# One written list for the first two units: sums, operands and combinations as steps of their own

## The chip, the cores and the metric

The kernel runs on one core of one Trainium2 chip. The metric is device time in microseconds, the median of three runs. A core has a matrix engine (TensorE, PE in the profile), a vector engine (VectorE, DVE), a scalar engine (ScalarE, ACT), a general engine (GpSimd, POOL) and a sync engine (SyncE, SP) whose queue issues most of the DMA transfers here. Each engine takes its instructions in the order in which the program lists them, and waits on semaphores where it needs another engine's result.

## The reference

Retention attention over 8 batches, 8 heads, 576 positions and head size 64, then an RMS norm and a SwiGLU feed-forward layer on the 4608 tokens of width 512 with inner width 1536, all in float32:

```python
scores = scale * np.matmul(q, k.transpose(0, 1, 3, 2))
Dmat = np.where(rel >= 0, gamma[:, None, None] ** rel[None, :, :], 0.0)
attn = np.matmul(scores * Dmat[None, :, :, :], v)
x = attn.transpose(0, 2, 1, 3).reshape(B * S, H * D)
rms = np.sqrt(np.mean(x * x, axis=-1, keepdims=True) + 1e-06)
xn = x / rms * rms_g
g = xn @ w_gate
out = (g * (1.0 / (1.0 + np.exp(-g))) * (xn @ w_val)) @ w_out
```

## The kernel before

**Units.** The 4608 tokens are worked in nine units of 512 (`NU`). Attention is done in 32 jobs, one for each batch and pair of heads; four jobs make a batch. Units 2 to 8 come from a loop after `start()`; units 0 and 1, with the loading, the attention of the first batches and the preparation of the weights, come from a list written out by hand, the string `PLAN`. `start()` first issues the loads in the order of `LOADS` (all on SP's queue), then walks through the list: `for step in PLAN.split(): tasks[step[0]](int(step[1:]))`. A step emits its instructions to whatever engines it uses; so the list sets the order on every engine, and nothing else does.

**Steps of the list.** For attention: `T` turns q and k of a job (transposes on PE, copies on ACT), `V` scales v, `S` is a job's slot (scores, states, weighing and, for the job before it, the outputs), `C` closes the last one, `P` and `F` prepare and fetch later jobs. For the norm: `Q` squares, `G` gathers, `N` the mean squares on PE (L454), `D` diagonals on ACT, `X` the `rb` matmul (L519) and four scalings on DVE (L521); for unit 2 `R`, `Y`, `X`, `M`: the `ms` matmul (L477), a root on ACT and DVE (L483 to L502), L521, and the four sums of x on DVE (L533) that the unit's second product needs (y, L614). For the weights: they come as 64-bit words and are brought to float32 in 36 halves; `a` is one exponent operation on ACT, `w` one step of a half (three DVE operations L1061, L1065, L1069, then a join L1086 on DVE); `W36` runs this to its end. Before slot 8 stands such a `W36`.

**The up projection.** `Uukn` is four 128x512 matmuls (L674) of unit u, set k, part n, followed by a silu on ACT or, for odd k, a multiply on DVE (L680). `d` makes two blocks of differences of h for the down projection on DVE (L698).

**The down projection.** `across(u)` multiplies h by the output weights with seven block products instead of eight, and each product again by seven. It is a generator: a first step that sets up, then for each product n an early step (three of the seven sub-products, with blocks taken from h directly, L773) and a late step (the other four), which needs four inner sums of that product's operand. After the late step the results in PSUM are kept (ACT, L788 and L790) or added (DVE, L800, L796) to the four output parts in `vec`. `A0` and `A1` each take one step of `across(0)` and `across(1)`.

**Inner sums.** `inner_sums(u, n)` makes them with four operations of 128x384 (L738, then three at L743), on POOL except where `on_vector` says DVE: products 4, 7, 10 and 12 when the two units' products are counted through as 7u + n. The buffer alternates with 7u + n, so the sums of a product can only start to overwrite when the late step two products earlier has been done. Before, those of product 7u + n + 2 are emitted by `across` itself, after the late step of product n and its adds; only products 0 and 1 of unit 0 are steps of the list, `i0` and `i1`.

**Operands and combination.** Two operands of the seven are sums of 128x1536 on DVE: the second and the last. Unit 0's are emitted at L937 and L943 behind its products 0 and 3, unit 1's at L955 and L957 behind unit 0's products 3 and 6. When unit 0 has had its seven products, its four output parts are combined at L977 by seven operations on all parts at once: parts 0 and 1 on DVE, 2 and 3 on POOL, 128x256 each. `o0` then stores unit 0's output (eight DMAs of 128 KB on SP).

Of the kernel before, what the change touches and what calls it, by code (L numbers as in the profile page):

```python
# [41 lines left out]
def kernel(  # L42
# [683 lines left out]
        at = (0, 1, None, 0, 1, 0, 1)[n] if u > 1 else (7 * u + n) % 2  # L726
        return [inner[:, at, i] for i in range(4)]

    def inner_sums(u, n, part=None):
# [4 lines left out]
        i1, i3, i2, i4 = inner_of(u, n)
        on_vector = u < 2 and 7 * u + n in (4, 7, 10, 12) or (u, n) == (NU - 1, 2)
        eng = nc.vector if on_vector else nc.gpsimd
        if part != 1:
            eng.tensor_tensor(out=i1, in0=x12, in1=x11, op=ALU.subtract)  # L738
        c = slice(1, NK) if part == 1 else slice(0, 1) if part == 0 else slice(0, NK)
        for o, a, b, op in (  # L740
            (i3, x22, x12, ALU.subtract), (i2, i3, x11, ALU.add), (i4, x21, i2, ALU.subtract),
        ):
            eng.tensor_tensor(out=o[:, c], in0=a[:, c], in1=b[:, c], op=op)  # L743
# [226 lines left out]
    def combine(b, eng=nc.vector):  # L970

        t = vec[:, b] if isinstance(b, slice) else vec[:, b : b + 1]
        for o, x, y in (
# [3 lines left out]
            eng.tensor_tensor(out=t[:, :, o], in0=t[:, :, x], in1=t[:, :, y], op=ALU.add)  # L977
# [147 lines left out]
    PLAN = """
        a1 a1 a1 a1 a1 T0 V0 S0 T1 V1 S1 a1 V2 T2 a1 Q0 V3 S2 G0 T3 Q1 a1 w1 a1 a1 S3 V4 a1 G1
        T4 w1 a1 S4 a1 a1 w1 a1 Q2 a1 a1 V5 T5 Q3 S5 G2 w1 V6 G3 w1 T6 S6 Q4 N0 D0 G4 V7 Q5 w1
        w1 T7 a1 a1 a1 X0 a1 G5 F8 S7 Q6 w1 U000 w1 G6 w1 C7 a1 a1 a1 a1 Q7 a1 G7 a1 a1 a1 a1 a1
        a1 w1 a1 a1 U001 N1 a1 a1 w1 U002 D1 w1 w1 U003 a1 w1 a1 X1 w1 w1 w1 U100 w1 w1 a1 U101
        a1 w1 w1 a1 a1 w1 a1 a1 w1 U010 w1 a1 U102 a1 w1 U103 a1 a1 w1 a1 w1 a1 w1 U011 a1 a1 w1  # L1130
        a1 w1 a1 w1 a1 a1 U012 w1 a1 w1 a1 w1 w1 a1 a1 U013 w1 a1 w1 U110 w1 w1 w1 U111 a1 a1 a1
        w1 a1 a1 w1 w1 a1 a1 w1 w1 a1 w1 U112 a1 a1 a1 a1 U020 a1 U113 a1 a1 a1 a1 a1 w1 w1 w1
        a1 U021 a1 w1 w1 a1 w1 w1 w1 U022 w1 a1 U120 w1 a1 w1 a1 a1 a1 w1 w1 w1 U121 a1 a1 U122
        a1 w1 U023 a1 U123 a1 w1 a1 a1 P8 a1 a1 a1 w1 w1 a1 a1 a1 w1 w1 w1 U030 w1 U031 F9 w1 a1
        w1 w1 a1 w1 U032 U130 a1 w1 a1 a1 U033 w1 w1 w1 a1 a1 a1 w1 a1 w1 w1 a1 w1 a1 U131 P9 a1
        a1 U132 a1 w1 U133 a1 w1 w1 w1 w1 w1 w1 U040 a1 U041 F10 w1 a1 w1 a1 a1 a1 a1 a1 a1 w1
        a1 U042 a1 w1 w1 a1 a1 a1 w1 U043 a1 w1 a1 a1 U050 a1 w1 w1 a1 a1 U051 U052 w1 w1 w1 w1
# [165 lines left out]
```

## Time and profile before

| what | value |
|---|---|
| runs | 1114.51, 1111.59, 1113.73 us, median 1113.73 |
| profiled execution | 1115.65 us, of which the span is 1113.8 |
| mean granted TensorE clock | 0.995 |
| instructions in the span | 24383 |
| HBM read, written | 212.05 MB, 30.08 MB |

The stretches by engine, from the table of windows of the profile: time in us that each engine was busy in each 25 us, with PE's granted clock.

| window, us | PE | DVE | ACT | POOL | PEclk |
|---|---|---|---|---|---|
| 0-25 | 20.25 | 10.27 | 12.41 | 0.87 | 1.00 |
| 25-50 | 20.35 | 18.10 | 14.85 | 0.35 | 0.93 |
| 50-75 | 24.39 | 20.07 | 14.48 | 5.96 | 0.93 |
| 75-100 | 24.16 | 16.53 | 14.94 | 6.37 | 1.00 |
| 200-225 | 23.70 | 23.33 | 6.31 | 13.77 | 1.00 |
| 250-275 | 25.00 | 22.58 | 5.00 | 18.02 | 1.00 |
| 275-300 | 23.69 | 21.64 | 4.13 | 19.62 | 1.00 |
| 300-325 | 24.09 | 17.79 | 4.04 | 13.22 | 1.00 |
| 350-375 | 23.01 | 16.38 | 4.11 | 5.93 | 0.93 |

The list's part takes the first 311 us or so: attention of the first batch and the loads up to about 58 us, the up projection of units 0 and 1 with the rounding of the weights and the slots of the second batch up to 240 us, unit 0's down projection from 240 to 278 us and unit 1's from 278 to 311 us. From there on the loop runs unit after unit. A window's busy time below 25 is time in which that engine stood still.

### The profile page before, as it was taken

How to read it: one execution, taken by the hardware profiler on the slowest of the kernel's cores; microseconds unless marked ns; L12 is line 12 of the kernel's file. 1: busy time of each engine (PE TensorE's matmuls, PEld its weight loads, DVE VectorE, ACT ScalarE, POOL GpSimd, SP SyncE). 2: the span in 40 equal slices, each digit the busy share in tenths (PEclk: the TensorE clock that was granted, in tenths of full speed). 3: DMA queues.
4: the chain of work that ended last, by engine and by line, in shares of the span. 5: the costliest groups of instructions: out<-in, count | busy, mean ns of one | idle time of the engine just before them, and what ended most of it. 6: DMA issues, size and time to landing. Idle time of an engine off the chain costs nothing.

```text
span 1113.8 us, 24383 instructions
## 1 busy us (share of the span) xinstructions
PE 1092.8 (98%) x10102; PEld 916.3 (82%) x10102; DVE 798.5 (72%) x1367; ACT 279.6 (25%) x565; POOL 467.6 (42%) x419
## 2 busy tenths in 40 slices
PE   8899999999999999999999999999999999999998
PEld 7654444469987899889988898889888998898888
DVE  4777767889867786688767785779476935594456
ACT  5557465211121220222022202131122111211110
POOL 0023535557730278025812382229312941393236
PEclk9899999999999999999999999999999999999999
DMA  7765889598778866787869865898485755575461
GB/s 183 202 183 198 307 210 258 196 330 227 235 286 225 189 224 244 214 223 212 290 166 215 275 251 171 245 229 293 154 216 199 248 208 177 171 287 169 157 245 42
DMA packets 253870, 243.72 MB, mean 219 GB/s; under 512 B 193088, under 2 KB 213824, under 8 KB 247616
## 3 DMA queue, kind: packets, MB, share of 16 engines
q1 hardware_dynamic: 252752, 241.87, 70.7%
q8 instruction: 79, 1.29, 0.5%
q10 hardware_dynamic: 1008, 0.30, 0.1%
q14 instruction: 31, 0.25, 0.1%
HBM read 212.05 MB, written 30.08 MB: 217 GB/s over the span
## 4 chain that ended last, share of the span: by engine, by line
PE 90%; DVE 5%; SPq 2%; issue 1%; POOL 1%; ACT 1%; DMA 0%; POOLq 0%; DVEq 0%; ACTq 0%
PE up L674 14%; PE x L614 13%; PE w L614 13%; PE z L614 13%; PE y L614 7%; PE xo L773 6%; PE xp L773 4%; PE zo L773 3%; PE zp L773 3%; PE yo L773 2%; PE wo L773 2%; PE av L355 2%; PE s L285 2%; PE av L375 2%; PE yp L773 1%
## 5 line engine op out<-in xcount | busy, mean ns | idle before, releaser
L674 PE MATMUL up<-x,ring 128*128 128x512 f32 x384 | 166.9, 594 | 1.3 <-DVE x L521 0.8
L614 PE MATMUL x<-x,ring 128*128 128x256 f32 x672 | 161.7, 384 | 0.0
L614 PE MATMUL w<-sums,ring 128*128 128x256 f32 x672 | 158.9, 379 | 0.0
L738 POOL TENSOR_TENSOR vi<-h 128x384 f32<-128x384 f32 x32 | 38.9, 1217 | 285.5 <-DVE h L633 270.2
L614 PE MATMUL z<-x,ring 128*128 128x256 f32 x672 | 158.8, 379 | 0.0
L674 PEld LDWEIGHTS up<-x,ring 128*128 128x128 f32 x384 | 72.4, 190 | 90.5 <-issue 84.1
L614 PEld LDWEIGHTS z<-x,ring 128*128 128x128 f32 x672 | 127.8, 190 | 19.8 <-issue 2.9
L614 PEld LDWEIGHTS w<-sums,ring 128*128 128x128 f32 x672 | 127.8, 190 | 17.2
L614 PEld LDWEIGHTS x<-x,ring 128*128 128x128 f32 x672 | 125.9, 191 | 17.5 <-issue 0.3
L743 POOL TENSOR_TENSOR vi<-h 128x384 f32<-128x384 f32 (+2 forms) x46 | 48.0, 1043 | 149.6 <-DVE h L633 149.6
L977 POOL TENSOR_TENSOR vi<-vi 128x512 f32<-128x512 f32 (+2 forms) x63 | 71.9, 1153 | 35.4 <-DVE vi L800 32.6
L640 ACT COPY m<-x 128x512 f32<-128x512 f32 x42 | 24.6, 585 | 231.1 <-PE x L614 231.1
L614 PE MATMUL y<-sums,ring 128*128 128x256 f32 x336 | 80.5, 383 | 0.9 <-DVE sums L533 0.9
L614 PEld LDWEIGHTS y<-sums,ring 128*128 128x128 f32 x336 | 64.7, 193 | 10.3 <-PE x L614 1.3
L621 DVE TENSOR_TENSOR h<-u,w 128x512 f32<-128x512 f32 x42 | 28.9, 688 | 58.5 <-PE w L614 58.2
L621 DVE TENSOR_TENSOR u<-m,y 128x512 f32<-128x512 f32 x42 | 28.7, 684 | 49.9 <-PE y L614 45.2
L635 ACT ACTIVATE h<-h 128x512 f32<-128x512 f32 x63 | 39.5, 629 | 82.1 <-DVE h L621 82.1
L334 DVE SCALAR_TENSOR_TENSOR sum<-sum,gc,s 128x64 f32<-128x64 f32 x192 | 53.9, 281 | 6.8
L1097 POOL TENSOR_TENSOR vi<-vi 128x512 f32<-128x512 f32 (+1 forms) x24 | 40.8, 1698 | 40.7 <-DVE vi L1086 26.8
L743 POOL TENSOR_TENSOR vi<-vi,h 128x384 f32<-128x384 f32 (+2 forms) x46 | 48.8, 1061 | 3.6
L743 POOL TENSOR_TENSOR vi<-h,vi 128x384 f32<-128x384 f32 (+2 forms) x46 | 46.2, 1005 | 3.6
L1097 POOL TENSOR_TENSOR ring<-ring 128x512 f32<-128x512 f32 x24 | 30.4, 1272 | 41.1 <-DVE ring L1086 30.7
(310 smaller groups left out, 2047.7 us busy)
## 6 DMA issues: line engine op xcount, KB each, us to landing
ring<-w_out_blocks SPq DMA_DIRECT2D x59, 1344.0 KB, 6.7
ring<-w_up_blocks SPq DMA_DIRECT2D x42, 1792.0 KB, 7.6
w_out_blocks<-vi SPq DMA_DIRECT2D x21, 448.0 KB, 4.5
out_dram<-vi SPq DMA_DIRECT2D x64, 128.0 KB, 3.1
qraw<-in_q_dram SPq DMA_DIRECT2D x96, 72.0 KB, 4.3
kraw<-in_k_dram SPq DMA_DIRECT2D x96, 72.0 KB, 3.4
k<-in_k_dram SPq DMA_DIRECT2D x48, 128.0 KB, 2.9
v<-in_v_dram SPq DMA_DIRECT2D x48, 128.0 KB, 3.1
```

The source lines that it names most:

```text
L285: nc.tensor.matmul(s[e][side(odd), i * L : i * L + L], lhsT=d["kT"][side(e), c * L : c * L + L], rhs=d["qT"][side(e), c * L : c * L + L], ...
L334: nc.vector.scalar_tensor_tensor(out=t[:, c], in0=t[:, c - 1], scalar=gc[:, hp : hp + 1], in1=part, op0=ALU.mult, op1=ALU.add,)
L614: nc.tensor.matmul(ps[:, i * HU : i * HU + HU], lhsT=w[:, PLACE[blk], c, i * P : i * P + P], rhs=t_of[u][blk][:, c], start=(start and i == ...
L621: nc.vector.tensor_tensor(out=o, in0=a, in1=pairs_of(ps), op=ALU.add)
L635: nc.scalar.activation(out=o, in_=c, func=AF.Silu)
L640: nc.scalar.copy(out=s1, in_=pairs_of(x_))
L674: nc.tensor.matmul(ps, lhsT=w[:, PLACE[blk], c % 2, i * P : i * P + P], rhs=x_of[u][:, c], start=(c == 0), stop=(c == NHP - 1),)
L738: eng.tensor_tensor(out=i1, in0=x12, in1=x11, op=ALU.subtract)
L743: eng.tensor_tensor(out=o[:, c], in0=a[:, c], in1=b[:, c], op=op)
L773: nc.tensor.matmul(ps, lhsT=lhs[:, c], rhs=w[:, s, c], start=((nm, s // 4) not in first), stop=False, skip_group_check=True,)
L977: eng.tensor_tensor(out=t[:, :, o], in0=t[:, :, x], in1=t[:, :, y], op=ALU.add)
L1097: nc.gpsimd.tensor_tensor(out=t[o], in0=t[x], in1=t[y], op=op)
```

## The change

What `across` emitted of its own for the first two units becomes steps of the list. `i` and `j` are now the inner sums of product n, counted 7u + n, on POOL and on DVE; `b0` and `b2` are the second operand of units 0 and 1, `b1` and `b3` the last one; `c` and `v` combine one output part of unit 0 on POOL and on DVE, with 128x128 operations. `combine` stores only where `late` is given, and `inner_sums` takes its engine as an argument; the work of units 2 to 8 is the same as before.

In the new list the inner sums of products 2, 6, 7, 8, 9, 10 and 11 are on DVE, those of 0, 1, 3, 4, 5, 12 and 13 on POOL. Parts 2, 0 and 3 of unit 0's output are combined on POOL, in this order, part 1 on DVE. Together DVE gains 12 operations of 128x384, and seven combining operations there are 128x128 instead of 128x256; POOL has 21 of 128x128 in place of seven of 128x256, and 12 inner sums fewer.

All other steps are set in a new order as well: the V, T, S steps of the first jobs, the U steps of both units, the a and w steps (two `a` fewer and one `w` more in the list, with the same instructions in all), the slots 8 to 11 against U043, U053 and U14n, and R2, Y2, X2, M2 of unit 2, where R2 stands after an early step instead of a late one's end. The loads have a new order too. In the diff the middle of both lists is left out.

```diff
@@ -726,14 +726,12 @@
         at = (0, 1, None, 0, 1, 0, 1)[n] if u > 1 else (7 * u + n) % 2
         return [inner[:, at, i] for i in range(4)]
 
-    def inner_sums(u, n, part=None):
+    def inner_sums(u, n, part=None, eng=nc.gpsimd):
 
         x = operands_of(u)[order_of(u)[n]]
         x11, x12 = x[:, :NK, :P], x[:, :NK, P:]
         x21, x22 = x[:, NK:, :P], x[:, NK:, P:]
         i1, i3, i2, i4 = inner_of(u, n)
-        on_vector = u < 2 and 7 * u + n in (4, 7, 10, 12) or (u, n) == (NU - 1, 2)
-        eng = nc.vector if on_vector else nc.gpsimd
         if part != 1:
             eng.tensor_tensor(out=i1, in0=x12, in1=x11, op=ALU.subtract)
         c = slice(1, NK) if part == 1 else slice(0, 1) if part == 0 else slice(0, NK)
@@ -741,6 +739,14 @@
             (i3, x22, x12, ALU.subtract), (i2, i3, x11, ALU.add), (i4, x21, i2, ALU.subtract),
         ):
             eng.tensor_tensor(out=o[:, c], in0=a[:, c], in1=b[:, c], op=op)
+
+    def second_operand(u):
+        o = operands_of(u)
+        nc.vector.tensor_tensor(out=o[S2], in0=o[A11], in1=o[S3], op=ALU.add)
+
+    def last_operand(u):
+        o = operands_of(u)
+        nc.vector.tensor_tensor(out=o[A22], in0=o[A12], in1=o[S2], op=ALU.subtract)
 
     def across(u):
 
@@ -882,7 +888,7 @@
                 inner_sums(u, n, part)
         if last:
             nc.vector.tensor_tensor(out=operands[S2], in0=b12, in1=b11, op=ALU.add)
-            inner_sums(u, 2)
+            inner_sums(u, 2, eng=nc.vector)
             nc.vector.tensor_tensor(out=operands[A22], in0=b21, in1=operands[S2], op=ALU.subtract)
         yield
         banks_in_turn = "zywxzwz" if u == 1 else "xxywzx." if last else "xzxzywx"
@@ -928,19 +934,21 @@
                 elif n == 4:
                     add(3, 3, "z")
                     add(2, 1, "z")
-                    combine(3)
+                    combine(3, late=True)
                 elif n == 5:
                     add(2, 2, "x")
-                    combine(2, nc.gpsimd)
+                    combine(2, nc.gpsimd, late=True)
             elif n == 0:
                 keep(1, "x")
-                nc.vector.tensor_tensor(out=b11, in0=b12, in1=b11, op=ALU.add)
+                if u:
+                    second_operand(u)
             elif n == 1:
                 keep(3, "z", -1.0)
             elif n == 2:
                 keep(0, "x")
             elif n == 3:
-                nc.vector.tensor_tensor(out=t1, in0=b21, in1=b11, op=ALU.subtract)
+                if u:
+                    last_operand(u)
             elif n == 4:
                 add(1, 1, "y")
                 add(2, 1, "z")
@@ -950,24 +958,15 @@
                 add(1, 1, "w")
             elif n == 6:
                 add(1, 1, "x")
-            o = operands_of(1)
-            if (u, n) == (0, 3):
-                nc.vector.tensor_tensor(out=o[S2], in0=o[A11], in1=o[S3], op=ALU.add)
-            elif (u, n) == (0, 6):
-                nc.vector.tensor_tensor(out=o[A22], in0=o[A12], in1=o[S2], op=ALU.subtract)
             if u > 1:
                 ahead = {0: 3, 1: 4, 2: 6, 3: 5} if last else {0: 3, 1: 4, 3: 5, 4: 6}
                 if n in ahead:
                     inner_sums(u, ahead[n])
-            elif 7 * u + n + 2 < 14:
-                inner_sums(*divmod(7 * u + n + 2, 7))
             yield
-        if not last:
-            if u == 0:
-                combine(slice(0, 2))
-            combine(slice(2, 4) if u == 0 else slice(0, 4), nc.gpsimd)
-
-    def combine(b, eng=nc.vector):
+        if u and not last:
+            combine(slice(0, 4), nc.gpsimd)
+
+    def combine(b, eng=nc.vector, late=False):
 
         t = vec[:, b] if isinstance(b, slice) else vec[:, b : b + 1]
         for o, x, y in (
@@ -975,7 +974,7 @@
             (S3, S1, S3), (A22, A11, A22),
         ):
             eng.tensor_tensor(out=t[:, :, o], in0=t[:, :, x], in1=t[:, :, y], op=ALU.add)
-        if not isinstance(b, slice):
+        if late:
             store(NU - 1, b)
 
     CORNERS = {A12: (0, 0), S4: (0, 1), S3: (1, 1), A22: (1, 0)}
@@ -1123,26 +1122,27 @@
     PLAN = """
-        a1 a1 a1 a1 a1 T0 V0 S0 T1 V1 S1 a1 V2 T2 a1 Q0 V3 S2 G0 T3 Q1 a1 w1 a1 a1 S3 V4 a1 G1
-        T4 w1 a1 S4 a1 a1 w1 a1 Q2 a1 a1 V5 T5 Q3 S5 G2 w1 V6 G3 w1 T6 S6 Q4 N0 D0 G4 V7 Q5 w1
-        w1 T7 a1 a1 a1 X0 a1 G5 F8 S7 Q6 w1 U000 w1 G6 w1 C7 a1 a1 a1 a1 Q7 a1 G7 a1 a1 a1 a1 a1
-        a1 w1 a1 a1 U001 N1 a1 a1 w1 U002 D1 w1 w1 U003 a1 w1 a1 X1 w1 w1 w1 U100 w1 w1 a1 U101
...
-        U053 a1 w1 w1 w1 a1 w1 a1 U140 W36 S8 a1 a1 a1 P10 U141 a1 S9 a1 a1 U142 F11 A0 a1 U143
-        a1 a1 a1 a1 z0 a1 d0 r1 a1 a1 a1 i0 d1 a1 S10 a1 a1 a1 P11 a1 a1 a1 U150 U151 a1 U152
-        S11 Q8 r2 U153 a1 i1 a1 d5 a1 d2 r99 A0 A0 A0 d3 C11 A0 A0 d4 G8 Q9 G9 A0 a1 A0 Q10 A0
-        k0 F12 G10 A0 A0 A0 a1 P12 A0 a1 A0 A0 F13 A0 Q11 G11 A1 A1 A1 o0 A1 A1 A1 A1 A1 A1 R2
-        A1 A1 A1 Y2 X2 M2 A1 a1 A1 A1 A1
+        V0 T0 a1 a1 a1 S0 T1 V1 a1 S1 T2 V2 a1 a1 V3 w1 S2 w1 Q0 T3 Q1 a1 G0 S3 a1 a1 V4 T4 a1
+        G1 a1 S4 a1 T5 a1 Q2 w1 G2 V5 w1 V6 Q3 S5 T6 a1 G3 a1 Q4 w1 V7 w1 S6 w1 F8 G4 N0 w1 a1
+        a1 D0 a1 T7 w1 a1 a1 a1 a1 X0 S7 a1 a1 a1 Q5 G5 w1 a1 Q6 G6 U000 a1 C7 Q7 w1 w1 a1 G7
+        U001 a1 N1 a1 w1 a1 D1 w1 w1 U002 a1 a1 a1 w1 a1 a1 a1 X1 w1 w1 w1 w1 a1 U003 a1 a1 a1
+        U100 w1 a1 w1 a1 w1 w1 w1 a1 w1 a1 a1 a1 a1 U110 a1 a1 w1 U101 w1 U010 w1 w1 w1 a1 w1 a1
...
+        U140 w1 a1 a1 a1 w1 a1 w1 a1 a1 a1 w1 a1 U043 U053 W36 S8 P10 U141 S9 a1 U150 a1 U142
+        F11 a1 a1 d0 a1 a1 Q8 z0 i0 a1 a1 U143 a1 S10 r1 a1 a1 U151 P11 U152 S11 U153 a1 d1 i1
+        d2 a1 a1 a1 Q9 r2 A0 r99 A0 A0 j2 A0 G8 a1 a1 d3 b0 d4 C11 A0 i3 A0 d5 a1 A0 a1 F12 A0
+        G9 b1 i4 Q10 k0 Q11 a1 b2 A0 i5 A0 a1 a1 G10 A0 j6 A0 A0 A0 a1 P12 A0 j7 b3 A0 j8 c2 A1
+        c0 F13 A1 v1 A1 c3 A1 j9 o0 G11 A1 A1 j10 A1 A1 j11 A1 i12 A1 R2 A1 Y2 A1 X2 M2 a1 a1
+        i13 A1 A1 A1 A1
     """
     TAILS = ((0, range(2)), (0, range(2, H)), (1, range(2)), (1, range(2, H)))
-    LOADS = [("table", 3), ("tails", 0), ("job", 0), ("job", 1), ("tails", 1), ("job", 2), ("job", 3), ("tails", 2), ("half", 0), ("job", 4), ("tails", 3), ("half", 1), ("job", 5), ("job", 6), ("half", 2), ("job", 7), ("half", 3), ("half", 4), ("rms_g", 0), ("table", 4)]
+    LOADS = [("tails", 0), ("job", 0), ("job", 1), ("tails", 1), ("tails", 2), ("job", 2), ("table", 3), ("job", 3), ("half", 0), ("half", 1), ("job", 4), ("tails", 3), ("job", 5), ("job", 6), ("job", 7), ("half", 2), ("half", 3), ("rms_g", 0), ("table", 4), ("half", 4)]
     stores = []
     n_joined = 0
     due = False
@@ -1222,7 +1222,11 @@
             "P": prepare, "F": fetch, "Q": lambda j: squares.append(squared(*divmod(j, NHP))),
             "G": lambda j: gather(*squares.pop(0)), "N": norm_1, "D": diagonals, "X": norm_2,
             "w": weights, "a": act, "d": lambda f: differences(f // 3, 2 * (f % 3)),
-            "i": lambda n: inner_sums(0, n), "z": lambda n: store_blocks(len(halves) + 9),
+            "i": lambda n: inner_sums(*divmod(n, 7)),
+            "j": lambda n: inner_sums(*divmod(n, 7), eng=nc.vector),
+            "c": lambda b: combine(b, nc.gpsimd), "v": combine,
+            "b": lambda n: (second_operand, last_operand)[n % 2](n // 2),
+            "z": lambda n: store_blocks(len(halves) + 9),
             "r": refill, "W": weights_to, "A": lambda u: next(outs[u], None), "R": root_1,
             "Y": root_2, "M": sums_of_x, "o": store,
             "k": lambda _: nc.vector.tensor_scalar(
```

The list without its a and w steps, from unit 0's last up products on, before:

```
U040 U041 F10 U042 U043 U050 U051 U052 U053 U140 W36 S8 P10 U141 S9 U142 F11 A0 U143 z0 d0 r1
i0 d1 S10 P11 U150 U151 U152 S11 Q8 r2 U153 i1 d5 d2 r99 A0 A0 A0 d3 C11 A0 A0 d4 G8 Q9 G9 ...
```

and after:

```
U040 F10 U133 U041 U042 U050 U051 U052 U140 U043 U053 W36 S8 P10 U141 S9 U150 U142 F11 d0 Q8 z0
i0 U143 S10 r1 U151 P11 U152 S11 U153 d1 i1 d2 Q9 r2 A0 r99 A0 A0 j2 A0 G8 d3 b0 d4 C11 A0 ...
```

More of the change, by code (lines that the diff above doesn't have):

```diff
@@ L1125 @@
     PLAN = """
-        a1 a1 a1 a1 a1 T0 V0 S0 T1 V1 S1 a1 V2 T2 a1 Q0 V3 S2 G0 T3 Q1 a1 w1 a1 a1 S3 V4 a1 G1
-        T4 w1 a1 S4 a1 a1 w1 a1 Q2 a1 a1 V5 T5 Q3 S5 G2 w1 V6 G3 w1 T6 S6 Q4 N0 D0 G4 V7 Q5 w1
-        w1 T7 a1 a1 a1 X0 a1 G5 F8 S7 Q6 w1 U000 w1 G6 w1 C7 a1 a1 a1 a1 Q7 a1 G7 a1 a1 a1 a1 a1
-        a1 w1 a1 a1 U001 N1 a1 a1 w1 U002 D1 w1 w1 U003 a1 w1 a1 X1 w1 w1 w1 U100 w1 w1 a1 U101
-        a1 w1 w1 a1 a1 w1 a1 a1 w1 U010 w1 a1 U102 a1 w1 U103 a1 a1 w1 a1 w1 a1 w1 U011 a1 a1 w1
@@ L1131 @@
[L1131 to L1136, printed above, removed]
@@ L1137 @@
-        a1 U042 a1 w1 w1 a1 a1 a1 w1 U043 a1 w1 a1 a1 U050 a1 w1 w1 a1 a1 U051 U052 w1 w1 w1 w1
-        U053 a1 w1 w1 w1 a1 w1 a1 U140 W36 S8 a1 a1 a1 P10 U141 a1 S9 a1 a1 U142 F11 A0 a1 U143
-        a1 a1 a1 a1 z0 a1 d0 r1 a1 a1 a1 i0 d1 a1 S10 a1 a1 a1 P11 a1 a1 a1 U150 U151 a1 U152
-        S11 Q8 r2 U153 a1 i1 a1 d5 a1 d2 r99 A0 A0 A0 d3 C11 A0 A0 d4 G8 Q9 G9 A0 a1 A0 Q10 A0
-        k0 F12 G10 A0 A0 A0 a1 P12 A0 a1 A0 A0 F13 A0 Q11 G11 A1 A1 A1 o0 A1 A1 A1 A1 A1 A1 R2
-        A1 A1 A1 Y2 X2 M2 A1 a1 A1 A1 A1
+        V0 T0 a1 a1 a1 S0 T1 V1 a1 S1 T2 V2 a1 a1 V3 w1 S2 w1 Q0 T3 Q1 a1 G0 S3 a1 a1 V4 T4 a1
@@ new lines @@
+        G1 a1 S4 a1 T5 a1 Q2 w1 G2 V5 w1 V6 Q3 S5 T6 a1 G3 a1 Q4 w1 V7 w1 S6 w1 F8 G4 N0 w1 a1
+        a1 D0 a1 T7 w1 a1 a1 a1 a1 X0 S7 a1 a1 a1 Q5 G5 w1 a1 Q6 G6 U000 a1 C7 Q7 w1 w1 a1 G7
+        U001 a1 N1 a1 w1 a1 D1 w1 w1 U002 a1 a1 a1 w1 a1 a1 a1 X1 w1 w1 w1 w1 a1 U003 a1 a1 a1
+        U100 w1 a1 w1 a1 w1 w1 w1 a1 w1 a1 a1 a1 a1 U110 a1 a1 w1 U101 w1 U010 w1 w1 w1 a1 w1 a1
+        w1 a1 U011 w1 a1 w1 a1 w1 w1 a1 a1 a1 w1 U111 a1 a1 w1 U012 w1 w1 w1 w1 a1 a1 a1 U102 w1
+        U112 a1 w1 w1 a1 U103 U013 a1 a1 a1 a1 w1 U020 w1 w1 a1 U021 a1 a1 a1 U120 w1 a1 w1 w1
@@ new lines @@
+        w1 a1 U022 a1 a1 w1 w1 a1 a1 a1 w1 a1 a1 a1 U113 w1 w1 U121 a1 a1 a1 w1 a1 w1 a1 w1 a1
+        w1 w1 w1 w1 U130 a1 P8 w1 U023 a1 w1 U122 a1 F9 U123 w1 a1 w1 a1 w1 a1 a1 a1 w1 a1 w1 w1
+        a1 a1 U030 U031 a1 a1 w1 w1 a1 a1 w1 a1 w1 U032 a1 U033 w1 U131 w1 w1 w1 w1 U132 a1 w1
+        w1 P9 a1 a1 a1 a1 a1 a1 w1 w1 a1 U040 F10 a1 w1 a1 U133 w1 a1 U041 a1 a1 a1 w1 a1 a1
+        U042 a1 w1 w1 w1 w1 w1 a1 a1 U050 w1 a1 a1 w1 a1 w1 a1 w1 w1 U051 U052 w1 w1 a1 w1 a1 a1
+        U140 w1 a1 a1 a1 w1 a1 w1 a1 a1 a1 w1 a1 U043 U053 W36 S8 P10 U141 S9 a1 U150 a1 U142
```

## The prediction

> **What bounds the kernel now.** I read the share of busy time first, then the chain of work that ended last, then the table of waits of PE (TensorE's matmul queue), and last the timelines around each wait. The first two say that PE is the bound nearly everywhere:
>
> ```profile
> PE 1092.8 (98%) x10102; PEld 916.3 (82%) x10102; DVE 798.5 (72%) x1367; ACT 279.6 (25%) x565; POOL 467.6 (42%) x419
> ...
> PE 90%; DVE 5%; SPq 2%; issue 1%; POOL 1%; ACT 1%; DMA 0%; POOLq 0%; DVEq 0%; ACTq 0%
> ```
>
> 1113.8 of span less 1092.8 leaves 21 us in which PE stands still. A change that takes no matmul away can win only from these, and from matmuls that crawl. Waits of PE (engine, line, waited for: us in total, times, longest):
>
> ```profile
> PE av L375 <- issue: 3.8, 2, 2.0
> PE turn_q L234 <- DMA h<-in_q_dram: 2.2, 1, 2.2
> PE turn_q L234 <- issue: 1.7, 1, 1.7
> ...
> PE y L614 <- DVE sums L533: 0.9, 1, 0.9
> PE up L674 <- DVE x L521: 0.8, 1, 0.8
> PE wp L773 <- POOL vi L743: 0.8, 2, 0.5
> ...
> PE last L305 <- DVE sums L1069: 0.6, 1, 0.6
> ...
> PE up L674 <- DVE vi L1086: 0.5, 1, 0.5
> ```
>
> Three sorts are to be seen: the start (DMA, issue), rounding on DVE that is late (L1069, L1086), and operand sums that are late (L743 on POOL, L533 on DVE). By windows of 25 us PE's idle time is 4.75 and 4.65 in the first 50 us, 1.3 in 200-225, 1.3 in 275-300, 0.9 in 300-325, 2.0 in 350-375, and near nothing elsewhere. The place that the change is named after is 275-300, in PE's timeline (start, duration, instruction, wait before it in brackets):
>
> ```profile
> 286.82 0.94 PE L773 MATMUL wo<-ring,vi 128*128 128x128 f32 x6 [0.17 <-POOL vi L738]
> 288.22 0.94 PE L773 MATMUL wp<-ring,vi 128*128 128x128 f32 x6 [0.47 <-POOL vi L743]
> 289.49 0.94 PE L773 MATMUL wp<-ring,vi 128*128 128x128 f32 x6 [0.33 <-POOL vi L743]
> 290.76 0.94 PE L773 MATMUL wo<-ring,vi 128*128 128x128 f32 x6 [0.34 <-POOL vi L743]
> ```
>
> This late step runs from 286.64 to 291.53, 4.89 us; its neighbours take 2.68. The inner sums come late because POOL stood in the combination, and DVE in its half, until 285.6 (POOL's, then DVE's timeline):
>
> ```profile
> 278.19 7.44 POOL L977 TENSOR_TENSOR vi<-vi 128x256 f32<-128x256 f32 x7
> 285.59 1.17 POOL L738 TENSOR_TENSOR vi<-ring 128x384 f32<-128x384 f32 x1
> ```
>
> ```profile
> 255.95 0.55 DVE L738 TENSOR_TENSOR vi<-h 128x384 f32<-128x384 f32 x1
> ...
> 279.77 6.14 DVE L977 TENSOR_TENSOR vi<-vi 128x256 f32<-128x256 f32 x7
> ...
> 287.24 1.34 DVE L738 TENSOR_TENSOR vi<-t 128x384 f32<-128x384 f32 x1
> ```
>
> The same inner-sum instruction takes DVE 0.55 us alone and 1.34 beside one of POOL: DVE and POOL don't add up.
>
> **What the Trainium skill says.** "SBUF — State Buffer", section "SBUF: two separate sides", says that DVE and GpSimd share one pair of ports as an exclusive lock, which an operation with two SBUF inputs holds for the whole instruction. The trace agrees: 0.55 against 1.34 above, while DVE's adds from PSUM (0.68, 0.55) don't stretch. "TensorE: Matmul & The Clock Gate", "Architectural detail", calls DVE's queue strictly first in, first out: what stands ahead of an inner sum is paid in full, as the 286 us wait shows. The same page, "What's actually happening", says that an idle window of about 3.4 us halves PE's clock; here waits of 1.8 and 2.0 us, among short matmuls, are already followed by windows with a granted clock of 0.93. "DMA: Bandwidth & Descriptors", "Issuing engines are not separate DMA queues", says that more issuers save only issue time; here SP issues nearly all loads at about 0.6 us each, so a load's place in the list is its cost.
>
> **The change part by part.** Gains are negative, against the profiled run's own 1115.65 (span 1113.8).
>
> 1. *Entrance of slot 8 (207.5-208.8): -1.3.* PE waits 0.59 and 0.46 for rounding of the weights and 0.26 inside the slot. Before, only U140's four matmuls (3.5 us) stand between U053 and S8, while DVE has 6.7 us of rounding between its multiply at 204.20 and the slot's L318 at 210.88. After, U140, U043 and U053 (10.65 us of PE) stand there, with 6.1 us of DVE work. 0.59 + 0.46 + 0.26 = 1.31.
>
> 2. *X1 (78.43): -0.84.* PE waits for L521, four operations (2.73 us), between the `rb` matmul and U100. After, U003 (3.5 us) stands between: covered.
>
> 3. *Product 2 of unit 1: -2.3.* Its inner sums go to DVE (j9), and the combination becomes one part of 128 columns on DVE (7 x 0.28 = 2.0 us, half of 256 columns' 6.14 / 7 with the neighbour's contention taken off) and three on POOL. 4.89 - 2.68 = 2.21, with restarts 2.3; by my count j9 is ready 0.2 to 0.5 us ahead.
>
> 4. *New wait, product 0 of unit 1: +1.3.* j7 was on DVE before too, but now behind j6 (four inner sums), the n=5 adds (2.14), P12's two transposes (1.43) and the n=6 adds (1.06), which wait for PE to end unit 0. Only the early step (2.01) lies between that end and the need. Counted from there: DVE's last add ends about 1.1 later, and j7's first result another 0.6 to 1.2; what j6 lost to contention earlier is added. With no contention PE waits about 0.2 to 0.7. POOL now runs 21 small operations from c2 on, 0.51 us each alone (7.44 / 7 halved), 0.65 beside DVE, 10.6 to 14 us in all, next to j6, j7, b3 and j8. I take 0.82 instead of 0.6 for j6's operations: a wait of 0.9, and 0.4 for sums that follow singly. Bounds +0.2 and +4. Behind j7 stand b3 (1.76 alone, 2.57 beside POOL) and j8: +0.1 more.
>
> 5. *Entrance of unit 2 (313.95): +0.8.* y waits 0.91 for L533. R2's `ms` matmul moves one early step (2.01) later on PE. DVE then no longer has inner sums ahead of L483 (they are on POOL), which gives back some 1.0 of it. Bounds +0.4 and +1.0.
>
> 6. *The loads of the first 58 us: -1.0.* The decay table leaves the head of SP's queue: the first q lands 0.39 earlier. Tails 2 (three issues) now stand ahead of job 2, and the table: job 2 1.25 later, job 3 about 1.3 later; half 1's 512 KB (2.3 us at 220 GB/s) ahead of job 4: slot 4 later by 1 to 2. Against it, T2, T5 stand ahead of V2, V5, so ACT's copies don't queue behind the scaling of v, V7 stands ahead of S6, and half 2 comes after job 7: slots 5 and 7 earlier, about 1.5 and 1. PE idles 9.4 us here, so there is room for either sign; bounds -3 and +2.5. The two issue waits (1.68 and 1.83) carry the clock with them and may move.
>
> 7. *At nothing:* the new orders of w, a and U between 78 and 205 us (DVE shows gaps of 2.15 and 2.75 at 195-199, PE no wait; if that cover fails, 0.7 to 2.7 for each late half of weights); b0-b3, the same four operations as at L937, L943, L955, L957, moved by one or two steps behind PE's early steps; o0's stores, which now wait for v1, hidden because their banks are needed some 5 us later; C11's 0.35, as before; units 2 to 8, whose work and order stay.
>
> Sum: -1.3 - 0.84 - 2.3 + 1.3 + 0.1 + 0.8 - 1.0 = -3.2. On the own time 1112.4; the three runs' median, 1113.73, stands 1.9 below the profiled one, so 1110.5.
>
> **The rivals.**
>
> *A. The combination on POOL starves DVE (slower).* Place: j6, j7, b3, j8 between 272 and 290 us. Each of POOL's 21 operations holds the ports some 0.24 us, 5.0 in all. If nearly all of it falls on the chain, parts 3-4 lose 0.7 + 5.0 instead of 1.4: 4.3 more, 1114.8. It decides from 3.2 us of blocking beyond mine, or inner sums of over 1.1 us on average. For it: 1.34 and 1.35 at 287. Against: POOL's new operations are a third as long as those there.
>
> *B. The start loses (slower).* Half 1 and tails 2 ahead of jobs 2-4 starve slots 2-4 by 2.0, and one more slow-clock window costs 1.75 (25 us at 0.93), in place of -1.0: 4.8 more, 1115.3. For it: job 4's loads are issued at 22.5-26.4 us, and its transposes run at 28 to 30, with little between. Against: the later slots gain.
>
> *C. Everything better.* j7 in time (+0.2 instead of 1.4) and the start at -2.8: 3.0 less, 1107.5. For it: the start's 9.4 us of idle.
>
> *D. The newly dealt weight steps leave PE waiting between 78 and 205 us.* Three halves late at 2.7 us: 8 more, 1118.5. Against: DVE's gaps.
>
> **How the numbers follow.** Forecast 0.38 (1108 to 1113), C 0.26, A 0.13, B 0.13, D 0.10. A measurement of this kernel tells about 0.3% (3.3 us) from no change, so 1110.4 and 1117.1 are the bounds. Half of the forecast and all of C are faster: 0.45. D, and a third of A and B, are slower: 0.19. The rest, 0.36, is the same. Range: from C less 2 to just beyond A and B, 1105.5 to 1117.5; D and the outer half of C's tail stay out.
>
> **What would show it.** Right: no wait on L1069 or L1086 at S8; none on L521 ahead of U100's place; the late step of unit 1's product 2 at about 2.7 us; a wait on DVE's inner sums at product 0 of unit 1 of about 1 us; y's wait near 1.7; the sum of PE's idle time in 0-58 us about 1 lower. Wrong: new waits of PE between 78 and 205, DVE's inner sums over 1.1 us beside the small POOL operations, or longer DMA waits in slots 2 to 4.

## The result, and the profile after

The changed kernel took 1109.94 us, the median of 11 runs (1107.34 to 1111.77), against 1113.73 for the kernel before (11 runs). The ratio is 0.9969, with a 95% interval from 0.9957 to 0.9982. A later set of six runs (e7 below) gave 0.9944 [0.9928, 0.9961]. By these two ratios the change gains 0.3 to 0.6%.

The profiled execution took 1110.56 us, with a span of 1108.6. From its page, busy time and the chain that ended last:

```profile
PE 1090.6 (98%) x10102; PEld 915.3 (83%) x10102; DVE 794.0 (72%) x1379; ACT 278.6 (25%) x565; POOL 458.0 (41%) x421
...
PE 93%; DVE 3%; SPq 1%; ACT 1%; issue 1%; DMA 1%; POOL 0%; POOLq 0%; ACTq 0%; DVEq 0%
```

PE still sets the end, and DVE's share of the chain has gone from 5 to 3%. PE's waits (engine, line, waited for: us in total, times, longest):

```profile
PE turn_q L234 <- issue: 2.3, 1, 2.3
...
PE y L614 <- DVE sums L533: 1.5, 1, 1.5
PE turn_q L234 <- DVE sum L334: 1.4, 1, 1.4
PE av L375 <- issue: 1.2, 1, 1.2
```

The waits for L1069, for the join, for L521 at X1 and for inner sums (then L743, now L741) are not in this table any more; y's wait has grown from 0.91 to 1.48. PE's timeline at the places that the prediction names (start, duration, instruction):

```profile
205.33 0.81 PE L285 MATMUL s<-qT,kT 64*64 64x64 f32 x40
...
206.54 3.70 PE L674 MATMUL up<-x,ring 128*128 128x512 f32 x8
...
275.04 0.85 PE L779 MATMUL zo<-ring,vi 128*128 128x128 f32 x6
275.73 1.62 PE L779 MATMUL zp<-ring,vi 128*128 128x128 f32 x12
277.19 0.89 PE L779 MATMUL zo<-ring,vi 128*128 128x128 f32 x6
277.92 1.50 PE L779 MATMUL yo<-ring,sums 128*128 128x128 f32 x12
...
284.77 0.83 PE L779 MATMUL wo<-ring,vi 128*128 128x128 f32 x6
...
287.45 1.50 PE L779 MATMUL xo<-ring,t 128*128 128x128 f32 x12
...
310.44 1.97 PE L614 MATMUL y<-sums,ring 128*128 128x256 f32 x8 [1.48 <-DVE sums L533]
```

The kernel before, at slot 8 and around product 2 of unit 1:

```profile
205.66 0.81 PE L285 MATMUL s<-qT,kT 64*64 64x64 f32 x40
...
208.31 3.70 PE L674 MATMUL up<-x,ring 128*128 128x512 f32 x8 [0.46 <-DVE vi L1086]
...
285.81 0.83 PE L773 MATMUL wp<-ring 128*128 128x128 f32 x6
...
291.53 1.50 PE L773 MATMUL xo<-ring,t 128*128 128x128 f32 x12
```

Slot 8's first part takes 206.54 - 205.33 = 1.21 us and took 208.31 - 205.66 = 2.65 before. The late step of unit 1's product 2 runs from 284.77 to 287.45, the full pace of 2.68. That of product 0, for which a wait was forecast, takes 277.92 - 275.04 = 2.88: no wait in brackets, only matmuls that are a little longer than 0.83 and 1.50. DVE in the changed kernel, at the same place:

```profile
267.11 0.55 DVE L736 TENSOR_TENSOR vi<-t 128x384 f32<-128x384 f32 x1
267.58 0.81 DVE L741 TENSOR_TENSOR vi<-t 128x384 f32<-128x384 f32 x1
268.50 0.63 DVE L741 TENSOR_TENSOR vi<-vi,t 128x384 f32<-128x384 f32 x1
269.16 0.69 DVE L741 TENSOR_TENSOR vi<-t,vi 128x384 f32<-128x384 f32 x1
269.78 0.68 DVE L806 TENSOR_TENSOR vi<-vi,wo 128x512 f32<-128x512 f32 x1
...
274.30 0.60 DVE L736 TENSOR_TENSOR vi<-x 128x384 f32<-128x384 f32 x1
...
281.86 1.99 DVE L976 TENSOR_TENSOR vi<-vi 128x128 f32<-128x128 f32 x7
```

and POOL:

```profile
267.27 14.25 POOL L976 TENSOR_TENSOR vi<-vi 128x128 f32<-128x128 f32 x21 [1.59 <-DVE vi L802]
```

j6's four operations (267.11 to 269.78) take 0.67 us each beside POOL's small ones. j7's first result is there at 274.30 + 0.60 = 274.90, and PE wants it at 275.04.

To compare runs I cut the span at four instructions of PE's timeline: U000 (the first matmul at L674), the first matmul of unit 0's down projection, the first of unit 2 (L614), and y. The parts between them in us, in all profiles of this study:

| kernel | start to U000 | U000 to down | down, units 0 and 1 | unit 2 to y | y to the end |
|---|---|---|---|---|---|
| before | 58.59 | 181.71 | 70.85 | 2.80 | 799.85 |
| changed | 59.37 | 178.87 | 68.83 | 3.37 | 798.16 |
| e7, changed again | 56.43 | 178.87 | 68.82 | 3.36 | 797.82 |
| e1, e10, old start | 58.99, 59.29 | 179.13, 179.12 | 68.84, 68.84 | 3.36, 3.36 | 797.88, 797.89 |
| e2, old middle | 55.80 | 181.71 | 68.83 | 3.36 | 797.90 |
| e3, old combination | 59.14 | 178.87 | 69.04 | 3.37 | 797.88 |
| e5, sums 9 on POOL | 55.23 | 178.86 | 69.29 | 3.36 | 798.26 |
| e8, wide combination | 59.69 | 178.86 | 71.35 | 3.37 | 798.33 |
| e4, root earlier | 56.82 | 178.87 | 69.56 | 2.50 | 798.05 |
| e9, wide and root | 58.96 | 178.86 | 71.36 | 2.34 | 797.38 |
| e6, e11, half 1 later | 55.86, 60.32 | 178.86, 178.86 | 68.81, 68.84 | 3.37, 3.37 | 797.80, 798.11 |
| e12, late sums at L802 | 57.64 | 178.86 | 68.83 | 1.73 | 798.24 |

The three columns in the middle repeat to 0.03 us for the same list. The first doesn't: with the changed kernel's start it lies between 55.23 and 59.69. The last has one outlier, the profile of before, in which an issue wait of 1.99 at 354.74 us was followed by a window with a clock of 0.93; the changed kernel's profile has there 1.24 and 1.00. In the rest of that column the profiles differ by up to 0.95. So the steady gain is read from the middle: 2.84 + 2.02 - 0.57 = 4.29 us; the start has to be read from medians.

### The profile page after: what moved, and what is told of

Its sections match the earlier page's. It is cut to its first block, busy times and chain, and to the rows that moved or that the text cites. A ratio compares the mean times of both kernels' runs of the same rounds, so it can differ in the third digit from the quotient of the medians.

```text
span 1108.6 us, 24401 instructions
## 1 busy us (share of the span) xinstructions
PE 1090.6 (98%) x10102; PEld 915.3 (83%) x10102; DVE 794.0 (72%) x1379; ACT 278.6 (25%) x565; POOL 458.0 (41%) x421
## 4 chain that ended last, share of the span: by engine, by line
PE 93%; DVE 3%; SPq 1%; ACT 1%; issue 1%; DMA 1%; POOL 0%; POOLq 0%; ACTq 0%; DVEq 0%
PE up L674 15%; PE x L614 13%; PE z L614 13%; PE w L614 13%; PE y L614 7%; PE xo L779 6%; PE xp L779 4%; PE zo L779 4%; PE zp L779 3%; PE yo L779 2%; PE wo L779 2%; PE av L355 2%; PE yp L779 2%; PE wp L779 2%; PE s L285 2%; PE av L375 1%
## 5 line engine op out<-in xcount | busy, mean ns | idle before, releaser
L674 PE MATMUL up<-x,ring 128*128 128x512 f32 x384 | 166.8, 594 | 0.0
L614 PE MATMUL x<-x,ring 128*128 128x256 f32 x672 | 160.8, 382 | 1.0 <-DVE t L698 1.0
L614 PE MATMUL w<-sums,ring 128*128 128x256 f32 x672 | 158.8, 379 | 0.0
L614 PE MATMUL z<-x,ring 128*128 128x256 f32 x672 | 158.7, 379 | 0.0
L674 PEld LDWEIGHTS up<-x,ring 128*128 128x128 f32 x384 | 72.4, 190 | 88.9 <-issue 85.6
L614 PEld LDWEIGHTS z<-x,ring 128*128 128x128 f32 x672 | 127.7, 190 | 19.9 <-issue 2.9
L614 PEld LDWEIGHTS w<-sums,ring 128*128 128x128 f32 x672 | 127.6, 190 | 17.4
L614 PEld LDWEIGHTS x<-x,ring 128*128 128x128 f32 x672 | 125.5, 190 | 18.2 <-issue 0.9
L741 POOL TENSOR_TENSOR vi<-h 128x384 f32<-128x384 f32 (+2 forms) x46 | 46.9, 1019 | 150.3 <-DVE h L633 150.3
L976 POOL TENSOR_TENSOR vi<-vi 128x512 f32<-128x512 f32 (+1 forms) x77 | 78.1, 1026 | 38.3 <-DVE vi L806 33.3
L614 PE MATMUL y<-sums,ring 128*128 128x256 f32 x336 | 79.5, 379 | 1.5 <-DVE sums L533 1.5
L614 PEld LDWEIGHTS y<-sums,ring 128*128 128x128 f32 x336 | 63.7, 190 | 10.6 <-issue 2.0
L334 DVE SCALAR_TENSOR_TENSOR sum<-sum,gc,s 128x64 f32<-128x64 f32 x192 | 53.9, 281 | 6.8
L1096 POOL TENSOR_TENSOR vi<-vi 128x512 f32<-128x512 f32 (+1 forms) x24 | 40.3, 1681 | 36.9 <-DVE vi L1085 14.8
L741 POOL TENSOR_TENSOR vi<-vi,h 128x384 f32<-128x384 f32 (+2 forms) x46 | 47.9, 1042 | 3.6
L318 DVE SCALAR_TENSOR_TENSOR ret<-s,causal 128x320 f32<-128x320 f32 x64 | 28.5, 484 | 27.4 <-PE s L285 26.8
```

Source lines behind the costliest of these rows:

```text
L318: nc.vector.scalar_tensor_tensor(out=ret[:, e], in0=s[e][:, : n * L].rearrange("p (c k) -> p c k", k=L), scalar=float(_gamma(H)[2 * hp + e ...
L334: nc.vector.scalar_tensor_tensor(out=t[:, c], in0=t[:, c - 1], scalar=gc[:, hp : hp + 1], in1=part, op0=ALU.mult, op1=ALU.add,)
L614: nc.tensor.matmul(ps[:, i * HU : i * HU + HU], lhsT=w[:, PLACE[blk], c, i * P : i * P + P], rhs=t_of[u][blk][:, c], start=(start and i == ...
L674: nc.tensor.matmul(ps, lhsT=w[:, PLACE[blk], c % 2, i * P : i * P + P], rhs=x_of[u][:, c], start=(c == 0), stop=(c == NHP - 1),)
L1096: nc.gpsimd.tensor_tensor(out=t[o], in0=t[x], in1=t[y], op=op)
```

## The experiments

All are the changed kernel with an edit. Where a line of the list is shown, only what differs is kept.

**e2: the list of before between U001 and W36.**

```diff
-        U002 ... X1 ... U003 ... U100 ... U140 ... U043 U053 W36
+        U002 ... U003 ... X1 ... U100 ... U043 ... U053 ... U140 W36
```

> The changed kernel with the kernel before's list between U001 and W36, so that only U140 stands between U053 and slot 8, and X1 is followed by U100 directly. If steps 1 and 2 of the prediction are right, the waits for L1069 and for the join at slot 8 and the wait for L521 at X1 come back, 0.9 + 1.7 us: 1112.5. If the new order gained something else in the stretch of rounding, more than 3.5 us; if it lost something there that the waits hide, less than 2.

Measured 1111.13 us (22 runs), 0.9979 [0.9970, 0.9988] of before. PE's waits:

```profile
PE up L674 <- DVE x L521: 0.8, 1, 0.8
...
PE last L305 <- DVE sums L1068: 0.6, 1, 0.6
...
PE up L674 <- DVE vi L1085: 0.5, 1, 0.5
```

The three waits are back at their old size, and the stretch from U000 to the down projection is 181.71 us, to the hundredth that of before. Steps 1 and 2 are shown, and together they are worth 2.84, more than the waits' brackets add up to (0.84 + 1.31). Slots 8 and 9 lost 1.44 + 0.29, and from the `rb` matmul of X1 to the next up product it was 1.86 instead of 0.86; a group of matmuls that has waited also starts slower (the groups of six at 286 to 291 us in the prediction's lines take 0.94 instead of 0.83). Some 0.1 us has no place.

**e3: unit 0's output combined as before, two parts each on DVE and POOL; inner sums as in the new list.**

```diff
-        j7 b3 A0 j8 c2 A1 c0 F13 A1 v1 A1 c3 A1 j9 o0
+        j7 b3 j8 A0 A1 F13 A1 A1 A1 j9 o0
+            if u == 0:
+                combine(slice(0, 2))
+            combine(slice(2, 4) if u == 0 else slice(0, 4), nc.gpsimd)
```

> The changed kernel with unit 0's output combined as before: two parts on DVE, two on POOL, behind product 6 of unit 0, and the inner sums where the new list has them. If step 3 is right (the combination is what held product 2's sums up), product 2's late step waits again: DVE has 6.1 us of combination ahead of j9, so 2.5 to 4 us slower than the changed kernel, 1112.5 to 1114. If moving product 9's sums to DVE was what helped, the late step stays at about 2.7 us and the kernel at 1110.

Measured 1110.23 us (6 runs), 0.9955 [0.9938, 0.9972]; product 2's late step takes 2.68 (284.75 to 287.43). DVE's timeline, then POOL's:

```profile
280.86 2.92 DVE L978 TENSOR_TENSOR vi<-vi 128x256 f32<-128x256 f32 x7
283.70 0.55 DVE L736 TENSOR_TENSOR vi<-ring 128x384 f32<-128x384 f32 x1
```

```profile
269.83 5.64 POOL L978 TENSOR_TENSOR vi<-vi 128x256 f32<-128x256 f32 x7 [4.39 <-DVE vi L806]
```

The old combination does no harm here. It took 6.14 us on DVE and 7.44 on POOL before because the two ran side by side; now POOL, with product 8's sums no longer ahead of it, starts as soon as DVE's adds for product 5 allow and has done its half by 275.5, and DVE's, alone, takes 2.92.

**e5: only product 9's sums back on POOL (`j9` becomes `i9`).**

> The changed kernel with only product 9's inner sums (unit 1's product 2) back on POOL, behind the 21 combining operations, which end at about 281.5 us. If the engine of these sums was all that mattered, the late step of product 2 waits again by about 2 us. If what mattered is that POOL and DVE no longer have inner sums of the product before and a combination in one queue ahead of them, POOL has them from 281.5 to 286 and the late step, which begins at 284.8, waits 0.5 us or less in all: time within 0.5 of the changed kernel's.

Measured 1111.28 us (3 runs), 0.9954 [0.9936, 0.9972]. POOL's timeline:

```profile
263.12 14.24 POOL L976 TENSOR_TENSOR vi<-vi 128x128 f32<-128x128 f32 x21 [1.60 <-DVE vi L802]
277.33 1.31 POOL L736 TENSOR_TENSOR vi<-ring 128x384 f32<-128x384 f32 x1
```

The sums are ready one by one from 278.6, the late step begins at 280.62 and takes 2.68. There is no wait for them. The 0.46 us that the down projection loses stand at product 4, whose first matmuls wait for ACT's copies of product 2; these start 1.0 us later than in the changed kernel. v1 on DVE takes 4.96 beside product 9's sums instead of 1.99, and unit 0's stores wait for v1; that these stores are what holds the copies up is likely, not shown.

So, with product 8's sums on DVE, neither the small combination nor product 9's engine was needed by itself. Before, POOL's queue held product 8's sums, the combination and product 9's sums (285.59) in one line:

```profile
273.33 1.28 POOL L738 TENSOR_TENSOR vi<-sums 128x384 f32<-128x384 f32 x1 [2.13 <-PE xo L773]
...
278.19 7.44 POOL L977 TENSOR_TENSOR vi<-vi 128x256 f32<-128x256 f32 x7
```

The change took the first and the last link out and cut the middle one up, so that its first part starts at 267.27. In every run of the changed list product 8's sums are off POOL. Whether that move alone would do is open: no run makes it alone, and none puts those sums back.

**e8: the combination as two lots of seven 128x256 operations on POOL.**

```diff
-            "c": lambda b: combine(b, nc.gpsimd), "v": combine,
+            "c": lambda b: combine(slice(b, b + 3, 2), nc.gpsimd),
-        j8 c2 A1 c0 F13 A1 v1 A1 c3 A1 j9
+        j8 c0 A1 c1 F13 A1 A1 A1 j9
```

> The changed kernel with unit 0's combination in two lots of seven 128x256 operations on POOL, parts 0 and 2 first, then 1 and 3, and none on DVE. In e3 POOL's seven took 5.6 us alone. Stores of unit 0 then begin at about 280.5 instead of 283.8, and ACT's copies of product 2 of unit 1 no longer wait for them; j9 is ready 2 us earlier. If DVE is held up for each POOL instruction as a whole, the sums of products 6 and 7 are slowed to 0.8 to 1.1 us as in e3, product 0's late step slips by 0.4 to 0.8, and the kernel is 0.5 slower than or equal to the changed one; if they suffer no more than beside 128x128, equal: 1109.9 within 0.5. By itself it isn't expected to gain.

Measured 1111.85 us (22 runs), 0.9975 [0.9964, 0.9987], and 71.35 in the down projection, 2.5 slower. DVE's timeline at j6, then PE's at the late steps of products 0 and 1:

```profile
267.41 0.55 DVE L736 TENSOR_TENSOR vi<-t 128x384 f32<-128x384 f32 x1
267.88 1.08 DVE L741 TENSOR_TENSOR vi<-t 128x384 f32<-128x384 f32 x1
269.07 0.90 DVE L741 TENSOR_TENSOR vi<-vi,t 128x384 f32<-128x384 f32 x1
270.00 0.97 DVE L741 TENSOR_TENSOR vi<-t,vi 128x384 f32<-128x384 f32 x1
270.90 0.67 DVE L806 TENSOR_TENSOR vi<-vi,wo 128x512 f32<-128x512 f32 x1
```

```profile
276.29 0.94 PE L779 MATMUL zo<-ring,vi 128*128 128x128 f32 x6 [0.78 <-DVE vi L736]
...
282.48 0.94 PE L779 MATMUL yo<-ring,vi 128*128 128x128 f32 x6 [0.25 <-DVE vi L736]
```

Now an inner sum takes (270.90 - 267.41) / 4 = 0.87 us, and product 0 waits as step 4 had it. This is rival A, and its switch is the width of POOL's operations beside these sums: larger pieces cost 2.5 us. POOL also has a fourth part to combine here, which keeps it busy to 283.0 instead of 281.5; but product 0's late step, which lost 1.8 of the 2.5, had ended at 280.1. Wide operations do no harm everywhere: in e3, where POOL's seven start behind j6 and run beside only the first two sums of j7, the down projection loses 0.2. My expectation bounded the slip at 0.8, from the first sum alone; the sums behind it, each held up again, made the rest.

**e4: R2 one early step earlier (`i12 R2 A1` for `i12 A1 R2`), and e9: the same on e8.**

> The changed kernel with R2 one early step earlier, where the kernel before has it, and product 12's sums still on POOL. If step 5 is right (R2's place sets the wait at y, 1.48 us), L483 begins some 1.1 to 2 us earlier and y waits 0 to 0.4: 1108.7. Rival: DVE's adds and the three sums at L802 stand ahead of L499 in the queue anyway, so that the wait stays above 1 and the time within 0.4 of 1109.9.

> The same with R2 one early step earlier. In e4 this took 0.87 off the wait at y and gave 0.73 back, since the ms matmul waited for a bank that ACT's late copies held. If the stores of unit 0 are what made these copies late, the 0.73 stays away here: from the first xo to y about 71.3 us against 72.2 in the changed kernel and in e4 72.06, and the kernel at 1109. If the copies are late for another reason, 72 and 1109.8.

e4 measured 1108.76 us (6 runs), 0.9954 [0.9942, 0.9966], e9 1110.87 (5 runs), 0.9965 [0.9953, 0.9977]. In e4, PE:

```profile
290.21 1.13 PE L477 MATMUL ms<-sq,ones 128*128 128x512 f32 x2 [0.46 <-ACT vi L794]
...
307.75 0.45 PE L614 MATMUL y<-sums,ring 128*128 128x256 f32 x1 [0.61 <-DVE sums L533]
```

and ACT, whose copies of unit 1's product 2 come before that:

```profile
288.71 0.58 ACT L794 COPY vi<-zo 128x512 f32<-128x512 f32 x1 [20.90 <-DMA out_dram<-vi]
```

R2's place makes most of the wait, as step 5 said: it falls by 0.87, in e9 by 1.03. I had expected 0 to 0.4 to be left, and 0.61 and 0.45 are. But the down projection gives 0.73 back in e4 (0.14 of gain is left, so the lower median is chance), since `ms` needs a bank that ACT frees late: the copies may not overwrite unit 0's output before it has been stored. In e9 nothing is given back, yet PE is 2.5 us later there anyway, so whether earlier stores would cure it stays open.

**e1 and e10: the loads and the list of before up to U001.**

```diff
-        V0 T0 a1 a1 a1 S0 T1 V1 a1 S1 T2 V2 ...
+        a1 a1 a1 a1 a1 T0 V0 S0 T1 V1 S1 a1 V2 T2 ...
-    LOADS = [("tails", 0), ("job", 0), ("job", 1), ("tails", 1), ("tails", 2), ("job", 2), ("table", 3), ...
+    LOADS = [("table", 3), ("tails", 0), ("job", 0), ("job", 1), ("tails", 1), ("job", 2), ("job", 3), ...
```

> The changed kernel with the kernel before's loads and its list up to and with U001. The traces say that the new start costs: U000 begins at 59.37 instead of 58.59. If job 4's late load is the cause, U000 comes back to about 58.6 and the kernel is 0.8 us faster than the changed one (1109.2 against 1109.9). If the prediction's ledger was right and the 0.8 is chance (an instruction-issue wait and the slow clock after it), it is 1.0 us slower (1110.9). Rival to both: the issue waits move with the list, and the difference is between -2 and +2 without any sign of the loads.

> The changed kernel with the old start once more. Step 6 of the prediction gave the new start 1.0 us, with bounds from 3 gained to 2.5 lost. If that is right, this kernel is about 1 us slower than e7 of the same set (e1 was 1.4 slower than the changed kernel, with intervals that overlap). If the start's order is nothing and chance is all, the two medians lie within 0.5.

e1 measured 1111.36 us (10 runs), 0.9975 [0.9964, 0.9986]; e10 1110.07 (5 runs), 0.9953 [0.9940, 0.9967]. Against the changed kernel (0.9969, and 0.9944 in e7, which ran beside e10) they are slower by 0.0006 and 0.0009, 0.7 and 1.0 us. Against e3 and e4 (0.9955 and 0.9954), which ran beside e1 and whose middle stretches sum to within 0.2 us of the changed kernel's, e1 is slower by 2.3. All these intervals overlap, and 0.26 of each difference lies behind U000 (179.13 against 178.87). U000 stands at 58.59, 58.99 and 59.29 in the three profiles with the old start, and at 57.7 in the mean of eight with the new one, spread over 4.5 us. My first reading of the two traces, that the new start costs 0.8, fell; that it gains 0.5 to 2 is likely, not shown.

**e6 and e11: half 1 loaded behind job 4, and e7, the changed kernel as their measure.**

```diff
-    ("half", 0), ("half", 1), ("job", 4), ("tails", 3), ...
+    ("half", 0), ("job", 4), ("half", 1), ("tails", 3), ...
```

> The changed kernel with half 1 loaded behind job 4 instead of ahead of it. If half 1's 512 KB delays slot 4 on the path, the transposes of job 4 begin 1 to 2 us earlier and the kernel is about 1 us faster: 1109. If the slots behind it absorb this (the start ends with the last jobs and the norm of unit 0), no change: 1109.9 within 0.7. Where U000 begins in one profile is no measure: with the same start it has stood between 55.8 and 59.4.

> e6 once more: half 1 behind job 4. If e6's 1.1 us of gain is real, this is about 1 us faster than e7; if it was chance, within 0.5.

> The changed kernel itself once more, on the chip and beside the runs of the three others of this set, as their measure: 1109.9 within 1, 0.997 of the kernel before. Its down projection (first xo to the first matmul of unit 2) 68.83 us and the wait at y 1.48 as in its first profile, since these don't hang on chance; U000 anywhere between 55 and 60.

e6 measured 1108.79 (0.9946 [0.9933, 0.9959]), e11 1109.51 (0.9956 [0.9942, 0.9969]), e7 1107.73 (0.9944), five to six runs each. Against the changed kernel the sign turns from one set to the other, and U000 stands at 55.86 and at 60.32. No effect of this load can be told from chance.

**e12: e6 with the three sums at L802 behind product 5's late step of unit 1.**

```diff
                 elif n == 4:
                     add(0, 0, "z")
+                elif n == 5:
                     for i in (2, 1, 3):
                         plus(i, 0)
-                elif n == 5:
                     add(2, 2, "w")
```

> e6 with one more edit, in unit 1's down projection: the three sums at L802 (3.1 us on DVE) are emitted behind product 5's late step instead of product 4's, so that they stand behind unit 2's L499 to L533 in DVE's queue. If the queue on DVE is what makes y late, L533 ends 3 us earlier and the wait of 1.48 is gone; ACT's copy of the last product and the copy of x behind it then wait for these sums and may hold PE by about 0.6: about 0.9 us faster than e6. If y doesn't hang on this queue, the wait stays.

Measured 1107.37 us (5 runs), 0.9934 [0.9921, 0.9946], the best ratio of all. PE's and DVE's timelines:

```profile
307.06 1.89 PE L614 MATMUL y<-sums,ring 128*128 128x256 f32 x8
308.79 1.89 PE L614 MATMUL z<-x,ring 128*128 128x256 f32 x8
310.75 1.99 PE L614 MATMUL x<-x,ring 128*128 128x256 f32 x8
```

```profile
305.45 0.69 DVE L533 TENSOR_TENSOR sums<-x,sums 128x512 f32<-128x512 f32 x1
306.06 3.09 DVE L802 TENSOR_TENSOR vi<-vi 128x896 f32<-128x896 f32 x3
```

y's wait is gone: L533 is done 0.9 us ahead of y, and the 3.09 us that stood in front of it now stand behind. 1.64 us are gained to y, and the fourth product starts 0.23 late (310.75 against 308.79 + 1.73), just after ACT's copy of the first product, which has come later. By these two it is 1.4 us faster than the changed kernel; by the medians of one set, 1107.37 against 1107.73, the two can't be told apart.

## Why the prediction was right, and where a term was off

The forecast of 1110.5 lies 0.6 from the median. By its steps:

1. Slots 8 and 9: -1.3 forecast, -1.73 measured (1.44 in slot 8, 0.29 in slot 9). Right; the brackets count the waits, not the slower restart.
2. X1: -0.84 forecast, -1.00 measured. Its wait is gone; with step 1 the stretch is worth 2.84 behind the new start (2.58 behind the old one, e1 and e10).
3. Product 2 of unit 1: -2.3 forecast. Right in size: the step went from 5.05 us (it could have begun at 285.81 + 0.67 = 286.48) to 2.68, -2.37. v1 took 1.99, as counted, and j9 was 0.46 ahead. The reason was too narrow. It named product 9's move and the smaller combination together; e3 and e5 show that either can be taken back without a wait. What made the wait was POOL's queue as a whole, and product 8's sums, which stood first in it, are not in the reason.
4. Product 0's new wait: +1.3 and +0.1 forecast, +0.20 and +0.15 measured. This term was mis-sized, by 1.05 us. The order in DVE's queue is as counted, but the floor was too high: 1.1 and 0.6 to 1.2 less 2.01 is at most 0.3, not 0.2 to 0.7, and in e3, with POOL idle beside j6, DVE even waited 0.38 for PE. And the price of j6's operations beside POOL's small ones was set at 0.82 and was 0.67. So DVE reached the n=6 adds at 273.25, 0.22 after PE had ended unit 0, and the early step's 2.01 us covered the rest, with 0.14 to spare. e8 shows that the wait is real at 0.87.
5. y: +0.8 forecast, +0.57 measured. Right; e4 shows R2's place, e12 that the queue ahead of L533 alone can end the wait.
6. The start: -1.0 forecast, between -0.7 and -2.3 by the comparisons of ratios, not settled. Job 4's transposes did come later (30.31 against 27.58), by more than the 1 to 2 counted, and the profile puts 1.37 of it to DVE's L334 and not to a load; at U000 0.78 of it was left. Longer waits for a load, which the prediction names as a sign of being wrong, came in three of the eight profiles with the new start: at about 20 us e7, e2 and e4 wait 1.4 to 1.8 for job 2's k. Yet these three have U000 at 55.80 to 56.82, ahead of every profile with the old start.
7. At nothing: the order between 78 and 205 us showed no wait, so rival D fell; the stores of o0 cost nothing at PE in the changed kernel. In units 2 to 8, whose order stays, most profiles with the new list have one wait of 0.3 to 1.0 for DVE's L698 (0.97 at 484.44 in the changed kernel's), and the one of before has none; it isn't in e4 and e9 either, and its cause is open.

Rival C came close: j7 was in time. Rival A's 0.24 us for each of POOL's operations has no working; each of j6's sums lost 0.12 beside them (0.67 against 0.55). Steps 1 to 5 sum to -2.24 as forecast and to -4.29 as measured: step 4 makes 1.05 of the difference, steps 1 and 2 make 0.70. With what the start gains the true gain is rather 5 than 3.8 us, which the second set (0.9944, 6.2 us) also suggests; that the first median lies so near the forecast is partly luck.

## What to carry to other kernels

Before you name the cause of a late result, write down everything that stands ahead of it in its engine's queue: here three links stood in line, the forecast named two, and each of the two could be taken back alone without a wait. If two engines slow each other, as DVE and POOL here, make the instructions of the one off the path small where they run beside the critical ones. And cut the trace at instructions that every version has: three of five stretches repeated to 0.03 us and showed effects of 0.2 us that the run times, spread over 4 us, could not.
